# Output sums of a dense expert layer in three PSUM tiles instead of one of four banks

## The chip, the core and the metric

The kernel runs on one NeuronCore of a Trainium2 chip. The metric is the device time of one execution in microseconds (us). TensorE (PE in the profile) multiplies matrices and adds into PSUM; VectorE (DVE), ScalarE (ACT) and GpSimd (POOL) do the element-wise work; SyncE (SP) issues most DMAs. Each engine runs its own instruction stream in order and waits on semaphores where it needs another engine's result.

## What is computed

A local attention over 1536 tokens feeds a routed layer of 8 experts, and its output feeds a second, dense layer of 4 experts. The change touches the step between the two layers and the second layer:

```python
# first layer, cut: each token goes to one of 8 experts
for e in range(8):
    mask = expert_idx == e
    h = np.maximum(x[mask] @ w1[e], 0.0)
    out[mask] = gate_w[mask, None] * (h @ w2[e])
# second layer: every token through all 4 experts
p = domain_probs / (domain_probs.sum(-1, keepdims=True) + 1e-09)
for e in range(4):                            # w1 512 x 1024, w2 1024 x 512
    h = np.maximum(x @ w1[e], 0.0)
    out += p[:, e:e + 1] * (h @ w2[e])
```

## The kernel before

**Tiling.** The tokens are 12 row tiles of 128. Every float32 factor is split into a high and a low part (`hi`, `lo`), so one product of two blocks is three matmuls. In the second layer an expert is cut into two halves of its hidden width and the tokens into three groups of four row tiles; a half with a group is a **unit**, and there are 4 x 2 x 3 = 24 of them, u = 0 to 23. Inside a unit both layers' 2 x 2 block products are made with 7 products instead of 8 (Strassen's way), which gives seven hidden products and seven output products. I call them **H u.j** and **S u.j**, j = 0 to 6. Each is 12 matmuls of 128x256: H at L1046 to L1048, S at L1124 to L1126.

**Order.** The seven H of unit 0 come first, alone. Then for every unit the loop alternates S u.0, H u+1.0, S u.1, H u+1.1, ... S u.6, H u+1.6, so that a product of one kind covers the element-wise work of the other. The seven S of the last unit come alone at the end, in `final`. The order on each engine is the order in which the code is written.

**Around an S product.** `weigh` multiplies the two 128x256 halves of its sum by the expert's probability and adds them to `acc` (the tile `xall`): two DVE instructions at L1030, or ACT instructions at L1033 where a block of `acc` is touched first. In the last unit `row_out` then sends a row tile out by an indirect DMA from POOL (L1036). `rest(j)` makes inputs that later S products need: s3 by L1060, low parts by L1054 and L1057.

**Around an H product.** `hidden` forms sums of the seven products: ACT copies (L1077, L1079, L1083) and relus (L1085, L1093), DVE additions (L1082, L1090, L1092), and the inputs of S (L1051 high parts, L1057 and L1054 low parts, L1060 relu with a sum, L1096 a difference). They all stand in DVE's and ACT's queues among the weighs. A unit's H products use three PSUM tiles of one bank each, and one more bank is `e`.

**The output sums.** One PSUM tile `yp` of four banks holds the output sums of both layers. The first layer uses it as four blocks of 512 outputs' sums. In the second, `zs` hands out its four banks in turn, three for each unit: x, y and z. S u.0 opens x, S u.1 opens y, S u.2 opens z; j = 3, 4 and 6 add to x again, j = 5 to z. Waits between engines are placed by tile: an instruction that writes any bank of `yp` waits for every earlier reader of `yp`.

**Between the layers.** `rows_in(e)` loads an expert's place in the row order into a register of ACT and DVE (L860), copies the first partial sums from `yp` to x2 on ACT (L864, two of 128x512) and adds the second ones on DVE (L866, two). For the last expert it is called between H 0.1 and H 0.2. `between` spreads the rest over the steps: parts of x for the H products of the first units (`x_parts`, ACT L833 and DVE L834, kept in DRAM by `x_keep` and read back by `x_back`), and the preparation of the next weights (ACT L156, POOL L157). `makes` is the table that says after which step which part of x is made.

Of the kernel before, what the change touches and what calls it, by code (L numbers as in the profile page):

```python
# [11 lines left out]
F32 = mybir.dt.float32  # L12
# [5 lines left out]
ALU = mybir.AluOpType  # L18
# [4 lines left out]
P = 128  # L23
# [6 lines left out]
CAP = 256  # L30
WIDTHS = 184, 232, 256
# [5 lines left out]
def tile_attention_moe_moe(ctx: ExitStack, tc: tile.TileContext, q, k, v, n_global, n_local,  # L37
# [771 lines left out]
    with ExitStack() as mo:  # L809
# [17 lines left out]
        def x_parts(c):  # L827

            b11, b12, b21, b22 = (x_block(c, a_, b_) for a_ in (1, 2) for b_ in (1, 2))
            ta, tb = (x_block(0, 1, 1), x_block(0, 1, 2)) if c else (b11, b11)  # L830

            def op(j, src):
                nc.scalar.activation(xo[:, j, 0], src, AF.Copy)  # L833
                nc.vector.tensor_tensor(xo[:, j, 1], src, xo[:, j, 0].bitcast(F32), ALU.subtract)  # L834

            def sub(o_, a_, b_, eng=nc.vector):
                eng.tensor_tensor(o_, a_, b_, ALU.subtract)

            sums = [lambda eng: sub(ta, b12, b11, eng), lambda eng: sub(b12, b22, b12, eng), lambda eng: sub(tb, b22, ta, eng)]
# [18 lines left out]
        def rows_in(e):  # L858

            o_ = nc.values_load(offi[0:1, e:e + 1], engines=(mybir.EngineType.Activation, mybir.EngineType.DVE),  # L860
                                min_val=max(0, NT - (NE - e) * CAP), max_val=min(NT, e * CAP))
            rows = [x2[:, d:d + 2, bass.ds(o_, CAP)] for d in range(0, KD, 2)]
            for d in range(2):
                nc.scalar.copy(rows[d], yp[:, 2 * d:2 * d + 2, 0, :])  # L864
            for d in range(2):
                nc.vector.tensor_tensor(rows[d], yp[:, 2 * d:2 * d + 2, 1, :], rows[d], ALU.add)  # L866

        with ExitStack() as m1:
            mp1 = m1.enter_context(tc.tile_pool(name="mp1", bufs=1))
# [58 lines left out]
            parts = gate(mp1, rsrc)  # L928
            sorted_ = {}

            (sa, sb, sc_), ops = x_parts(0)
            first_parts = [ops[0], lambda: sa(nc.vector), lambda: sb(nc.vector), ops[1], lambda: sc_(nc.vector)] + ops[2:]
            xparts = {c: x_parts(c) for c in range(1, NCH)}

            def side(st):
# [34 lines left out]
            for e in range(NE):  # L970
                xa, xb = (xh, xl) if e else (xh0, xl0)
                for i in range(4):
                    st = 8 * e + i
                    wh, wl = use(st)
                    pt = next(hp)
                    for w_ in two_widths(wide) if e else (CAP,):
                        for f in range(2):
                            ws = slice(f * P, (f + 1) * P)
                            for c in range(KD):
                                o_, a_, b_ = pt[:, f, 0:w_], xa[:, c, 0:w_], xb[:, c, 0:w_]  # L980
                                nc.tensor.matmul(o_, wh[:, c, ws], a_, start=c == 0, stop=False)  # L981
                                nc.tensor.matmul(o_, wh[:, c, ws], b_, start=False, stop=False)
                                nc.tensor.matmul(o_, wl[:, c, ws], a_, start=False, stop=c == KD - 1)
                    relu3(pt, hhl[:, 2 * i:2 * i + 2, 0, :], hhl[:, 2 * i:2 * i + 2, 1, :])
                    split_to(min(st + PRE, W0))
                    side(st)
                    if st == 1:
                        nc.vector.memset(yp[:, :, :, WIDTHS[0]:], 0.0)
                for i in range(4):
                    st = 8 * e + 4 + i  # L990
                    wh, wl = use(st)
                    for f in range(2):
                        kf = 2 * i + f
                        for w_ in three_widths(wide):
                            a_ = hhl[:, kf, :, 0:w_]
                            for d in range(KD):
                                ws = slice(d * P, (d + 1) * P)
                                nc.tensor.matmul(yp[:, d, :, 0:w_], wh[:, f, ws], a_, start=kf == 0, stop=False, skip_group_check=True)  # L998
                                nc.tensor.matmul(yp[:, d, 0, 0:w_], wl[:, f, ws], a_[:, 0], start=False, stop=kf == KF - 1, skip_group_check=True)  # L999
                    if e + 1 < NE and i < 2:  # L1000
                        flip_x(e + 1, i)
                    if e + 1 < NE and i == 2:
                        ahead = wider(e + 1)
                    if i == 2 and e + 2 < NE:
                        load_x(e + 2)
                    split_to(min(st + PRE, W0))
                    side(st)
                wide = ahead
                if e < NE - 1:
                    rows_in(e)  # L1010


        with ExitStack() as m2:
            np1 = m2.enter_context(tc.tile_pool(name="np1", bufs=1))
            zs = cycle([yp[:, d] for d in range(KD)])
            LAST = 2 * NE2 - 1
            NU = NCH * 2 * NE2
            HT = CH // 2
# [43 lines left out]
            class Unit:  # L1062
# [65 lines left out]
                def second(self):  # L1128

                    n, t0 = self.n, self.t0  # L1130
                    t1_ = t0 + HT
                    x_, y_, z_ = (next(zs) for _ in range(3))
                    prods = ((x_, t0, 0), (y_, t0, 0), (z_, t1_, 1), (x_, t0, 1), (x_, t1_, 1), (z_, t0, 1), (x_, t1_, 0))
                    for j, (pt, t_, d_) in enumerate(prods):
                        for i in range(HT):
                            self.product(j, pt[:, i], i, j < 3 and i == 0)
                        for i in range(HT):
                            weigh(n, t_ + i, d_, pt[:, i])
                            if n == LAST and j > 4:
# [34 lines left out]
            def between(u, j):  # L1174

                n, c = divmod(u, NCH)
                if (u, j) in makes:
                    x_, m = makes[u, j]
                    xparts[x_][1][m]()
                    x_keep(x_, m)  # L1180
                if u == 0 and 4 <= j:
                    xparts[2][0][j - 4](nc.gpsimd)
                if u < 0 and j in (1, 4, 5, 6):
                    w2_op(0, j if j > 3 else 3)
# [222 lines left out]
```

## Time and profile before

| | us |
|---|---|
| median of three runs | 810.64 |
| lowest and highest | 809.51, 811.54 |
| the profiled execution | 807.23 |
| its span, first to last instruction | 805.2 |

All rows of the trace come from the profiled execution; 2.03 us of it lie outside the span. A row of the timeline gives the start, the duration, the engine, the line, what was written and read, and in brackets how long the engine had been idle before and what ended that. TensorE's matmuls overlap: one starts 0.12 us after another though each is recorded as 0.28 us, so "idle" begins later than the first possible start of the next. [...]

### The profile page before, as it was taken

How to read it: one execution, taken by the hardware profiler on the slowest of the kernel's cores; microseconds unless marked ns; L12 is line 12 of the kernel's file. 1: busy time of each engine (PE TensorE's matmuls, PEld its weight loads, DVE VectorE, ACT ScalarE, POOL GpSimd, SP SyncE). 2: the span in 40 equal slices, each digit the busy share in tenths (PEclk: the TensorE clock that was granted, in tenths of full speed). 3: DMA queues.
4: the chain of work that ended last, by engine and by line, in shares of the span. 5: the costliest groups of instructions: out<-in, count | busy, mean ns of one | idle time of the engine just before them, and what ended most of it. 6: DMA issues, size and time to landing. Idle time of an engine off the chain costs nothing. (4 is left out here: it accounts for less than half of the span.)

```text
span 805.2 us, 16423 instructions
## 1 busy us (share of the span) xinstructions
PE 756.6 (94%) x6267; PEld 729.5 (91%) x6267; DVE 561.3 (70%) x1186; ACT 427.7 (53%) x861; POOL 340.9 (42%) x313
## 2 busy tenths in 40 slices
PE   8999999999999888899999999999999999999983
PEld 5888899999999788899999999999999999999983
DVE  7888677778876577766667667667677667677652
ACT  7899477666755467653443453443454444354320
POOL 2036520340002663563564555356366266255252
PEclk9999999999999999999999999999999999999998
DMA  7986375676664754864566456466566466554602
GB/s 227 322 287 223 116 251 207 216 236 238 229 221 159 278 194 163 321 221 167 201 232 214 161 211 215 173 236 235 184 236 229 160 220 228 184 179 160 213 27 81
DMA packets 44418, 166.20 MB, mean 206 GB/s; under 512 B 5208, under 2 KB 11624, under 8 KB 36256
## 3 DMA queue, kind: packets, MB, share of 16 engines
q1 hardware_dynamic: 41888, 158.44, 55.9%
q0 software_dynamic: 2416, 6.39, 2.2%
q8 instruction: 66, 1.08, 0.5%
q14 instruction: 32, 0.26, 0.1%
q10 hardware_dynamic: 16, 0.02, 0.0%
HBM read 143.29 MB, written 21.54 MB: 205 GB/s over the span
## 5 line engine op out<-in xcount | busy, mean ns | idle before, releaser
L1124 PE MATMUL y<-wt,hp 128*128 128x256 f32 x672 | 193.1, 287 | 32.7 <-DVE xall L1030 19.9
L1030 DVE SCALAR_TENSOR_TENSOR xall<-y,rsb,xall 128x256 f32<-128x256 f32 x312 | 136.5, 479 | 108.1 <-PE y L1126 107.4
L1046 PE MATMUL h<-xo,wt 128*128 128x256 f32 x672 | 190.4, 283 | 3.0 <-ACT hf L1083 2.5
L1047 PE MATMUL h<-xo,wt 128*128 128x256 f32 x672 | 190.2, 283 | 0.0
L1125 PE MATMUL y<-wt,hp 128*128 128x256 f32 x672 | 190.1, 283 | 0.0
L1126 PE MATMUL y<-wt,hp 128*128 128x256 f32 x672 | 190.1, 283 | 0.0
L1048 PE MATMUL h<-xo,wt 128*128 128x256 f32 x672 | 190.0, 283 | 0.0
L157 POOL TENSOR_TENSOR wt<-raw,wt 128x512 fp32r<-128x512 f32 x75 | 98.0, 1307 | 166.1 <-ACT wt L156 164.6
L1124 PEld LDWEIGHTS y<-wt,hp 128*128 128x128 f32 x672 | 128.6, 191 | 39.3 <-ACT wt L156 12.6
L1046 PEld LDWEIGHTS h<-xo,wt 128*128 128x128 f32 x672 | 129.0, 192 | 3.4 <-ACT hf L1083 2.7
L1047 PEld LDWEIGHTS h<-xo,wt 128*128 128x128 f32 x672 | 129.0, 192 | 0.0
L1048 PEld LDWEIGHTS h<-xo,wt 128*128 128x128 f32 x672 | 129.0, 192 | 0.0
L1125 PEld LDWEIGHTS y<-wt,hp 128*128 128x128 f32 x672 | 128.8, 192 | 0.0
L1126 PEld LDWEIGHTS y<-wt,hp 128*128 128x128 f32 x672 | 128.8, 192 | 0.0
L1051 ACT ACTIVATE hp<-hf 128x512 fp32r<-128x512 f32 x120 | 75.4, 628 | 69.4 <-DVE hf L1060 68.0
L1054 DVE TENSOR_TENSOR hp<-hf,hp 128x512 fp32r<-128x512 f32 x92 | 87.2, 948 | 0.0
L998 PE MATMUL y<-hhl,wh 128*128 128x368 f32 (+2 forms) x256 | 80.6, 374 | 0.0
L94 DVE TENSOR_TENSOR wl<-raw,wh 128x1024 fp32r<-128x1024 f32 x60 | 72.6, 1225 | 0.1
L1093 ACT ACTIVATE hf<-h 128x512 f32<-128x512 f32 x24 | 14.3, 598 | 102.2 <-DVE h L1092 102.2
L124 ACT ACTIVATE wh<-raw 128x1024 fp32r<-128x1024 f32 x59 | 61.9, 1058 | 12.6 <-DMA raw<-in_moe_w_dram 10.6
L999 PE MATMUL y<-hhl,wl 128*128 128x184 f32 (+2 forms) x256 | 66.7, 261 | 0.0
L981 PE MATMUL h<-xh,wh 128*128 128x232 f32 (+1 forms) x224 | 61.9, 276 | 0.0
(217 smaller groups left out, 1488.4 us busy)
## 6 DMA issues: line engine op xcount, KB each, us to landing
raw<-in_moe_w_dram SPq DMA_DIRECT2D x96, 512.0 KB, 4.4
xo<-xd SPq DMA_DIRECT2D x42, 1024.0 KB, 5.2
xo<-xd SPq DMA_DIRECT2D x21, 1536.0 KB, 6.3
xd<-xo SPq DMA_DIRECT2D x21, 512.0 KB, 2.9
xs<-zt SPq DMA_DIRECT2D x4, 1024.0 KB, 6.2
xr<-xs SPq DMA_DIRECT2D x14, 256.0 KB, 4.8
v<-in_v_dram SPq DMA_DIRECT2D x12, 256.0 KB, 4.5
k<-in_k_dram SPq DMA_DIRECT2D x11, 256.0 KB, 5.0
```

What stands on the lines that cost most here:

```text
L94: eng.tensor_tensor(lo, r, hi.bitcast(F32), ALU.subtract)
L157: eng.tensor_tensor(t[:, 1], src, t[:, 0].bitcast(F32), ALU.subtract)
L998: nc.tensor.matmul(yp[:, d, :, 0:w_], wh[:, f, ws], a_, start=kf == 0, stop=False, skip_group_check=True)
L1030: nc.vector.scalar_tensor_tensor(a_, src, w_, a_, ALU.mult, ALU.add)
L1046: nc.tensor.matmul(pt[:, i], wh[:, d, ws], xh_[:, d], start=new and i == d == 0, stop=False, skip_group_check=True)
L1047: nc.tensor.matmul(pt[:, i], wh[:, d, ws], xl_[:, d], start=False, stop=False, skip_group_check=True)
L1048: nc.tensor.matmul(pt[:, i], wl[:, d, ws], xh_[:, d], start=False, stop=d == 1, skip_group_check=True)
L1051: nc.scalar.activation(parts[i][0], src, func)
L1054: eng.tensor_tensor(parts[i][1], src, parts[i][0].bitcast(F32), ALU.subtract)
L1124: nc.tensor.matmul(pt, hh[:, f, ts_], wh[:, f], start=new and f == 0, stop=False, skip_group_check=True)
L1125: nc.tensor.matmul(pt, hh[:, f, ts_], wl[:, f], start=False, stop=False, skip_group_check=True)
L1126: nc.tensor.matmul(pt, hl[:, f, ts_], wh[:, f], start=False, stop=f == 1, skip_group_check=True)
```

## The change

The tile `yp` becomes three: `ya` with two banks, `y2` and `y3` with one each; the first layer still uses all four banks. In the second layer units take turns: an even unit has x in `ya`, y in `y2`, z in `y3`, an odd one x in `y2`, y in `ya`. The second bank of `ya` is then unused. In `final` the last unit's x is held in two tiles of the H pool.

`rows_in` is split into `place`, `rows_copy` and `rows_add`, and each of the last two now has three instructions (one of 128x512, two of 128x256) instead of two. For the last expert the place is loaded before its second half, the copies stay after H 0.1, and the additions come after H 0.2. The memset of unused columns becomes four. The subtraction in the seventh part of x becomes a step of its own, on POOL for two of the three groups; `makes` and the preparation of weights in unit 0's H products are dealt out anew.

```diff
-        yp = ps_y.tile([P, KD, 2, CAP], F32, name="y")
+        ya = ps_y.tile([P, 2, 2, CAP], F32, name="ya")
+        yp = [ya[:, 0], ya[:, 1], *(ps_y.tile([P, 2, CAP], F32, name=f"y{d}") for d in (2, 3))]
...
-            ops = [lambda: op(0, b11), lambda: op(1, ta), lambda: op(2, tb), lambda: op(3, b21), lambda: op(4, b12),
-                   lambda: op(5, b22), lambda: (sub(b21, b21, tb), op(6, b21))]
+                    lambda eng: sub(b21, b21, tb, eng)]
+            ops = [lambda: op(0, b11), lambda: op(1, ta), lambda: op(2, tb), lambda: op(3, b21), lambda: op(4, b12),
+                   lambda: op(5, b22), lambda: op(6, b21)]
...
-            for d in range(2):
-                nc.scalar.copy(rows[d], yp[:, 2 * d:2 * d + 2, 0, :])
-            for d in range(2):
-                nc.vector.tensor_tensor(rows[d], yp[:, 2 * d:2 * d + 2, 1, :], rows[d], ALU.add)
+        ys = (0, 2, ya), (2, 3, yp[2].unsqueeze(1)), (3, 4, yp[3].unsqueeze(1))
+
+        def rows_copy(o_):
+            for d0, d1, y_ in ys:
+                nc.scalar.copy(x2[:, d0:d1, bass.ds(o_, CAP)], y_[:, :, 0, :])
+
+        def rows_add(o_):
+            for d0, d1, y_ in ys:
+                rows = x2[:, d0:d1, bass.ds(o_, CAP)]
+                nc.vector.tensor_tensor(rows, y_[:, :, 1, :], rows, ALU.add)
...
+                if e == NE - 1:
+                    last_place = place(e)
...
-            zs = cycle([yp[:, d] for d in range(KD)])
...
-                    x_, y_, z_ = (next(zs) for _ in range(3))
+                    x_, y_, z_ = (yp[2], yp[0], yp[3]) if self.u % 2 else (yp[0], yp[2], yp[3])
...
-                    x_ = [next(zs)[:, 0] for _ in range(HT)]
-                    y_, z_ = (next(zs) for _ in range(2))
+                    xa, _, xb = (ps_h.tile([P, 2, HC], F32, tag="h", name="h") for _ in range(3))
+                    x_ = [xa[:, 0], xb[:, 0]]
+                    y_, z_ = yp[2], yp[3]
...
-            makes = {}
-            for x_ in (1, 2):
-                for m in range(7):
-                    makes[(-1, 2 * m + 3) if x_ == 1 and m < 2 else (0, m + 5) if m < 2 else (x_ - 1, m - 2)] = x_, m
+            makes = {(-1, 3): [(1, 0)], (-1, 6): [(1, 1)], (0, 0): [(1, 2)], (0, 1): [(1, 3)], (0, 2): [(1, 4), (1, 5)], (0, 3): [(1, 6), (2, 0)],
...
                 if j == 1:
-                    rows_in(NE - 1)
+                    rows_copy(last_place)
+                if j == 2:
+                    rows_add(last_place)
```

On TensorE, at the boundary between unit 4 and unit 5 (end of H 5.6, start of S 5.0), the order before, with the semaphores that an instruction waits on; `h` is an H tile, `hp110` and `hp111` are the high and low part of h11, the input of S u.0:

```order
L1046 MATMUL h_6938<-xo_1742,wt_6486 128x256
L1047 MATMUL h_6938<-xo_1742,wt_6486 128x256
L1048 MATMUL h_6938<-xo_1742,wt_6486 128x256
L1124 MATMUL y_1737<-wt_6524,hp110_5806 128x256 [waits DVE_49,Activation_49]
L1125 MATMUL y_1737<-wt_6524,hp110_5806 128x256
L1126 MATMUL y_1737<-wt_6524,hp111_5807 128x256 [waits Pool_49]
```

The same place after:

```order
L1058 MATMUL h_6959<-xo_1744,wt_6507 128x256
L1059 MATMUL h_6959<-xo_1744,wt_6507 128x256
L1060 MATMUL h_6959<-xo_1744,wt_6507 128x256
L1136 MATMUL y2_1738<-wt_6545,hp110_5836 128x256 [waits Activation_49]
L1137 MATMUL y2_1738<-wt_6545,hp110_5836 128x256
L1138 MATMUL y2_1738<-wt_6545,hp111_5837 128x256 [waits Pool_49]
```

No instruction moves; the first S matmul of a unit no longer waits on DVE's semaphore.

On ACT, around the last expert's rows between H 0.1 and H 0.2, before (`hf_5800` and `hf_5801` are copies of H sums, `x` is x2, `offi` the experts' places):

```order
L1079 COPY hf_5801<-h 128x512
L860 TENSOR_LOAD offi
L860 ISA x2
L864 ISA
L864 COPY x_1741<-y 128x2x256
L864 ISA
L864 COPY x_1741<-y 128x2x256
L156 ACTIVATE wt<-raw 128x512
L1083 COPY hf_5800<-h 128x512
```

After:

```order
L1091 COPY hf_5831<-h 128x512
L868 ISA
L868 COPY x_1743<-ya 128x2x256
L868 ISA
L868 COPY x_1743<-y_1738 128x256
L868 ISA
L868 COPY x_1743<-y_1739 128x256
L156 ACTIVATE wt<-raw 128x512
L1095 COPY hf_5830<-h 128x512
```

The load of the place has gone from here to an earlier point, and a third copy stands ahead of the copy that follows H 0.2's partial sum.

On DVE at the same place, before (L1082 adds H 0.2's partial sum to H 0.0's):

```order
L866 ISA
L866 TENSOR_TENSOR x_1741<-y,x_1741 128x2x256
L866 ISA
L866 TENSOR_TENSOR x_1741<-y,x_1741 128x2x256
L1082 TENSOR_TENSOR h<-h,hf_5800 128x512
L834 TENSOR_TENSOR xo<-x_1741,xo 128x512
L1090 TENSOR_TENSOR e<-h,hf_5801 128x512
```

After:

```order
L1094 TENSOR_TENSOR h<-h,hf_5830 128x512
L873 ISA
L873 TENSOR_TENSOR x_1743<-ya,x_1743 128x2x256
L873 ISA
L873 TENSOR_TENSOR x_1743<-y_1738,x_1743 128x256
L873 ISA
L873 TENSOR_TENSOR x_1743<-y_1739,x_1743 128x256
L835 TENSOR_TENSOR xo<-x_1743,xo 128x512
L1102 TENSOR_TENSOR e<-h,hf_5831 128x512
```

The additions of the rows have moved behind the addition of the partial sum.

## Rows read from the trace of the kernel before

**Rows 1.** The page, busy time of TensorE: us (share of span) and instructions.

```profile
PE 756.6 (94%) x6267; PEld 729.5 (91%) x6267; DVE 561.3 (70%) x1186; ACT 427.7 (53%) x861; POOL 340.9 (42%) x313
```

**Rows 2.** Busy time by stretch: start:end, length, engines' busy us (instructions), clock, DMA.

```profile
108.00:268.00 160.00, 160.00 (x1241) 156.12 (x1240) 123.08 (x156) 105.07 (x155) 26.04 (x19) 1.00 0.64 214
...
267.90:374.67 106.77, 93.91 (x758) 91.30 (x757) 69.40 (x105) 59.65 (x115) 60.24 (x44) 1.00 0.62 231
374.67:778.68 404.01, 387.33 (x3192) 384.02 (x3193) 278.29 (x495) 173.88 (x313) 200.60 (x153) 1.00 0.55 199
778.68:796.58 17.90, 11.72 (x84) 10.41 (x84) 6.94 (x15) 2.03 (x4) 9.29 (x9) 1.00 0.16 60
```

**Rows 3.** Timeline at the start of S 5.0: start, us, engine, line, [idle before].

```profile
393.57 0.69 DVE L1060 SCALAR_TENSOR_TENSOR hf<-e,hf 128x512 f32<-128x512 f32 x1 [0.67 <-ACT hf L1093]
...
394.30 0.69 DVE L1096 TENSOR_TENSOR hf<-hf,hf 128x512 f32<-128x512 f32 x1
...
394.65 0.28 PE L1047 MATMUL h<-xo,wt 128*128 128x256 f32 x1
...
394.77 0.28 PE L1048 MATMUL h<-xo,wt 128*128 128x256 f32 x1
...
394.91 0.87 DVE L1030 SCALAR_TENSOR_TENSOR xall<-y,rsb,xall 128x256 f32<-128x256 f32 x2
...
395.36 0.58 ACT L1051 ACTIVATE hp<-h 128x512 fp32r<-128x512 f32 x1
...
395.92 0.35 PE L1124 MATMUL y<-wt,hp 128*128 128x256 f32 x1 [0.88 <-ACT hp L1051]
395.97 0.69 DVE L1057 SCALAR_TENSOR_TENSOR hp<-h,hp 128x512 fp32r<-128x512 f32 x1 [0.19 <-ACT hp L1051]
```

**Rows 4.** What TensorE waited for, 374.67 to 776: total us, times, longest.

```profile
PE y L1124 <- ACT hp L1051: 8.8, 10, 0.9
PE y L1124 <- DVE xall L1030: 7.9, 9, 0.9
```

**Rows 5.** The same list, 268 to 374.

```profile
PE y L1124 <- DVE xall L1030: 5.0, 6, 1.6
PE y L1124 <- ACT xall L1033: 4.0, 4, 1.3
PE h L1046 <- ACT hf L1083: 2.5, 1, 2.5
PE h L1046 <- DVE e L1090: 0.6, 1, 0.6
```

**Rows 6.** Timeline around the last expert's rows, before H 0.4.

```profile
272.55 1.07 ACT L864 COPY x<-y 128x512 f32 x2 [0.97 <-issue]
...
273.65 1.29 DVE L866 TENSOR_TENSOR x<-y,x 128x512 f32 x2 [5.65 <-ACT x L864]
...
274.86 0.69 DVE L1082 TENSOR_TENSOR h<-h,hf 128x512 f32<-128x512 f32 x1
...
276.27 0.38 PE L1046 MATMUL h<-xo,wt 128*128 128x256 f32 x1 [2.45 <-ACT hf L1083]
```

**Rows 7.** Instructions that read tile y, ACT at L1033: duration min/median/max in ns.

```profile
L1033 ACT ACTIVATE xall<-y,rsb x24: 454/467/477, 285.0 to 352.9; 128x256 f32<-128x256 f32 x24
```

**Rows 8.** What TensorE waited for, 776 to 800.

```profile
PE y L1124 <- DVE xall L1030: 7.1, 7, 1.1
```

**Rows 9.** Timeline of the end: POOL's row_outs, the last matmul, the last weigh.

```profile
784.19 0.99 POOL L1036 DMA_INDIRECT out_dram<-xall,rsb  x1 [0.15 <-issue]
785.49 0.98 POOL L1036 DMA_INDIRECT out_dram<-xall,rsb  x1 [0.30 <-issue]
...
796.30 0.28 PE L1126 MATMUL y<-wt,hp 128*128 128x256 f32 x1
796.62 0.48 DVE L1030 SCALAR_TENSOR_TENSOR xall<-y,rsb,xall 128x256 f32<-128x256 f32 x1 [1.79 <-PE y L1126]
...
798.66 0.98 POOL L1036 DMA_INDIRECT out_dram<-xall,rsb  x1 [0.31 <-POOLq L1226]
```

More of the change, by code (lines that the diff above doesn't have):

```diff
@@ L837, in sub @@
                 eng.tensor_tensor(o_, a_, b_, ALU.subtract)
-            sums = [lambda eng: sub(ta, b12, b11, eng), lambda eng: sub(b12, b22, b12, eng), lambda eng: sub(tb, b22, ta, eng)]
+            sums = [lambda eng: sub(ta, b12, b11, eng), lambda eng: sub(b12, b22, b12, eng), lambda eng: sub(tb, b22, ta, eng),
+                    lambda eng: sub(b21, b21, tb, eng)]
             ops = [lambda: op(0, b11), lambda: op(1, ta), lambda: op(2, tb), lambda: op(3, b21), lambda: op(4, b12),
-                   lambda: op(5, b22), lambda: (sub(b21, b21, tb), op(6, b21))]
+                   lambda: op(5, b22), lambda: op(6, b21)]
             return sums, ops
@@ L856, in relu3, with place @@
             nc.vector.scalar_tensor_tensor(lo, pt, 0.0, hi.bitcast(F32), ALU.max, ALU.subtract)
[L858 to L862, printed above, removed]
-            for d in range(2):
-                nc.scalar.copy(rows[d], yp[:, 2 * d:2 * d + 2, 0, :])
-            for d in range(2):
-                nc.vector.tensor_tensor(rows[d], yp[:, 2 * d:2 * d + 2, 1, :], rows[d], ALU.add)
+        def place(e):
+            return nc.values_load(offi[0:1, e:e + 1], engines=(mybir.EngineType.Activation, mybir.EngineType.DVE),
+                                  min_val=max(0, NT - (NE - e) * CAP), max_val=min(NT, e * CAP))
+        ys = (0, 2, ya), (2, 3, yp[2].unsqueeze(1)), (3, 4, yp[3].unsqueeze(1))
[6 more added lines that the diff above has]
+                nc.vector.tensor_tensor(rows, y_[:, :, 1, :], rows, ALU.add)
         with ExitStack() as m1:
@@ L929, in tile_attention_moe_moe @@
             sorted_ = {}
-            (sa, sb, sc_), ops = x_parts(0)
-            first_parts = [ops[0], lambda: sa(nc.vector), lambda: sb(nc.vector), ops[1], lambda: sc_(nc.vector)] + ops[2:]
+            sums_, ops = x_parts(0)
+            sums_ = [lambda f=f: f(nc.vector) for f in sums_]
+            first_parts = [ops[0], *sums_[0:2], ops[1], sums_[2], *ops[2:4], sums_[3], *ops[4:]]
             xparts = {c: x_parts(c) for c in range(1, NCH)}
@@ L987, in tile_attention_moe_moe @@
                     if st == 1:
-                        nc.vector.memset(yp[:, :, :, WIDTHS[0]:], 0.0)
+                        for y_ in yp:
+                            nc.vector.memset(y_[:, :, WIDTHS[0]:], 0.0)
+                if e == NE - 1:
+                    last_place = place(e)
                 for i in range(4):
@@ L997, in tile_attention_moe_moe @@
                                 ws = slice(d * P, (d + 1) * P)
-                                nc.tensor.matmul(yp[:, d, :, 0:w_], wh[:, f, ws], a_, start=kf == 0, stop=False, skip_group_check=True)
-                                nc.tensor.matmul(yp[:, d, 0, 0:w_], wl[:, f, ws], a_[:, 0], start=False, stop=kf == KF - 1, skip_group_check=True)
+                                nc.tensor.matmul(yp[d][:, :, 0:w_], wh[:, f, ws], a_, start=kf == 0, stop=False, skip_group_check=True)
+                                nc.tensor.matmul(yp[d][:, 0, 0:w_], wl[:, f, ws], a_[:, 0], start=False, stop=kf == KF - 1, skip_group_check=True)
                     if e + 1 < NE and i < 2:
@@ L1009, in tile_attention_moe_moe @@
                 if e < NE - 1:
-                    rows_in(e)
+                    o_ = place(e)
+                    rows_copy(o_)
+                    rows_add(o_)
         with ExitStack() as m2:
             np1 = m2.enter_context(tc.tile_pool(name="np1", bufs=1))
-            zs = cycle([yp[:, d] for d in range(KD)])
             LAST = 2 * NE2 - 1
@@ L1176, in between @@
                 n, c = divmod(u, NCH)
-                if (u, j) in makes:
-                    x_, m = makes[u, j]
+                for x_, m in makes.get((u, j), ()):
                     xparts[x_][1][m]()
                     x_keep(x_, m)
[L1181 to L1184, printed above, removed]
+                if u in (0, 1) and j == 2:
+                    xparts[u + 1][0][3](nc.gpsimd)
+                if u == 0 and 3 <= j < 6:
+                    xparts[2][0][j - 3](nc.gpsimd)
+                if u < 0:
+                    for m in {1: (3,), 4: (4,), 6: (5, 6)}.get(j, ()):
+                        w2_op(0, m)
                 if NCH <= u + 2 < NU and j in (2, 4, 6):
@@ L1202, in between @@
                     w1_op(n + 1, 6)
-            makes = {}
-            for x_ in (1, 2):
-                for m in range(7):
-                    makes[(-1, 2 * m + 3) if x_ == 1 and m < 2 else (0, m + 5) if m < 2 else (x_ - 1, m - 2)] = x_, m
+            makes = {(-1, 3): [(1, 0)], (-1, 6): [(1, 1)], (0, 0): [(1, 2)], (0, 1): [(1, 3)], (0, 2): [(1, 4), (1, 5)], (0, 3): [(1, 6), (2, 0)],
+                     (0, 4): [(2, 1)], (1, 0): [(2, 2)], (1, 1): [(2, 3)], (1, 2): [(2, 4)], (1, 3): [(2, 5)], (1, 4): [(2, 6)]}
             unit = Unit(0)
```

## The prediction

> **What bounds the kernel now.** I read the page's shares first, then busy time by stretch, then the list of what TensorE waited for in each stretch, and single boundaries in the timeline last. TensorE is busy 94% of the span [rows 1]; where the rest goes is told by the stretches [rows 2]. In the first layer (108 to 268) TensorE is busy 160.00 of 160 us, at clock 1.00: nothing can be won there. The second layer is cut at its first matmul (267.90), at the first matmul of S 4.0 (374.67) and at that of S 23.0 (778.68). Two matmuls in a row start 0.12 us apart (394.65, 394.77 [rows 3]), so a product of 12 takes 1.44 us and the matmuls alone set a floor for each stretch:
>
> - head, 267.90 to 374.67: 106.77 us for 63 products = 756 matmuls x 0.12 = 90.72. Lost: 16.05.
> - steady part, 374.67 to 778.68: 404.01 us for 19 units of 168 matmuls, 383.04. Lost: 20.97, or 1.10 a unit.
> - tail, 778.68 to the last matmul's start at 796.30 [rows 9]: 17.62 us for 83 steps of 0.12, 9.96. Lost: 7.66.
>
> Together 44.68 us: all that a change of TensorE's waits can win.
>
> Who ends the waits? In the steady part there are 19, one for each unit, all ahead of an S product, 0.88 us each [rows 4]. The list puts ten of them down to ACT's L1051, but at S 5.0 that instruction runs from 395.36 to 395.94 and the matmul starts at 395.92 [rows 3]: it can't be the cause. The weigh of S 4.6 can: DVE does it from 394.91 to 395.78, 0.14 before the matmul. It is late because it stands in DVE's queue behind L1060 and L1096 (393.57 to 394.99), which make inputs from H 5.5. S 5.0 writes another bank than the weigh reads, but the same tile, so it waits. The listing of TensorE before shows that wait on DVE; the listing after does not have it. S 5.0 could start at 394.89; it starts 1.03 later, and its first matmul takes 0.20 to the next instead of 0.12, together the 1.10.
>
> In the head ten waits out of twelve are of the same kind, 9.0 us of idle [rows 5]; one, 2.5 us, is that of H 0.4, one, 0.6, that of H 0.6. The idle time, 12.1 us, is less than the loss of 16.05, since a wait costs about 0.22 more than its idle (0.88 against 1.10) and short delays leave no idle at all. In the tail seven S products run with no H between, and each waits for the weigh before it, 7.1 us [rows 8].
>
> **The change, part by part.**
>
> Steady part. Between units the wait for the weigh of S u-1.6 goes: S u.0 now opens a tile that was last read by the weigh of S u-1.1, a whole unit ago. What is late next? S u.1 opens the tile that S u-1.6 used and waits for that same weigh: it ends at 395.78, and S 5.1 would start at 394.89 + 2.88 = 397.77, so 2.0 are to spare. S u.3, u.4 and u.6 write x again and wait for the weigh of x's product before. From the last matmul's start to the end of its weighs it takes 0.32 + 0.87 (796.30 to 796.62 [rows 9], and the pair in [rows 3]) = 1.19; an H product of 1.44 lies between, and so S may start 1.56 after that matmul: 0.37 to spare. In the trace every S u.1 to u.6 has this wait already, since all banks are one tile, and none of the 19 waits stands there. Next is DVE's own row. With t0 = 394.77, the last matmul of H 5.6: weighs to 395.78, L1057 395.97 to 396.66, another L1060 to 397.34, the weighs of S 5.0 (0.87) to 398.2, L1060 for s3 to 398.9 at the latest; H 6.1, which takes over the PSUM tile that s3 is made from, would start at 394.89 + 3 x 1.44 = 399.21. That leaves 0.3 to 0.55, so nothing is lost as long as these rows keep their length. DVE is busy 278.29 us in the stretch [rows 2], and 383.04 remain. I take the whole 20.97; at the least half, 10.5, if that row comes up short by 0.55 in each unit.
>
> Tail. The order there is j = 0, 1, 2, 3, 5, 4, 6. Each product waits for a weigh that lies at least two products back, but for S 23.6, which adds to x right behind S 23.4; there x's two halves have a tile each, and the weigh of the one (0.48) can run under the matmuls of the other. TensorE would take 9.96 plus little. But POOL follows: its row_outs start 1.30 apart (784.19, 785.49), the first two don't depend on the last unit's sums, and with four more at that distance the last starts at 784.19 + 5 x 1.30 = 790.69 and not at 798.66 [rows 9]. That wins 7.97. The weighs keep up: the last product would end near 787.8, its weighs near 788.9, and the row_outs that need them stand at 789.39 and 790.69. Of the 7.97, S 23.0's own late start (1.03) is already in the steady part's sum. The tail gives 6.9; the ends are 6 and 7.6.
>
> Head. The ten waits for weighs and the short delays cost 16.05 less 2.8 for H 0.4 and 0.8 for H 0.6, 12.4. They go as in the steady part, but ACT does some of these weighs, among parts of x that the new table packs closer (two in one step, twice); I leave 0.4 for S 0.4 and 1.1 for the rest: 10.9 won. H 0.4 waits for a chain: 0.97 of ACT's idle for the load of the place, two copies, DVE's two additions (273.65 to 274.94), L1082 behind them, a copy on ACT, then the matmul at 276.27 [rows 6]. H 0.3 is through 2.6 us earlier. After the change the load is gone from here and L1082 stands ahead of the additions; what remains is a third copy on ACT and a weight's preparation, so about 0.5 of 2.8 stays: 2.3 won. The wait of H 0.6 stays. Head: 13.2; the ends are 10 and 15.
>
> Small parts. Three copies and three additions instead of two: a 128x256 copy from this tile takes 467 ns on ACT [rows 7] and one of 128x512 some 540 in a row (1.07 for two [rows 6]), so 0.4 more on ACT; on DVE 2 x 0.48 for 0.65, 0.3 more. For seven experts this lies in the first layer, where ACT is busy 105.07 and DVE 123.08 of 160 us [rows 2]: taken at nothing, at most 7 x 0.3 = 2 if TensorE waited for it each time, and the early load of the place at most its 0.97. Four memsets for one, and a subtraction that moves to POOL: nothing, POOL being busy 60.24 of 106.77 in the head.
>
> The sum: 20.97 + 6.9 + 13.2 = 41.1. On the profiled execution 807.23 - 41.1 = 766.1. The median of the three runs is 3.41 above that execution, so **769.5**.
>
> **The rivals.**
>
> B, the wait moves inside the unit. If DVE's row or the weigh of x is late by the 0.3 to 0.5 that I count as spare, H u.1 or S u.4 waits in each of 20 units; with half of the boundary's gain lost: 769.5 + 10.5 = 780. For it: the slack is thinner than one DVE instruction (0.69). Against it: all instructions of that row are of one length wherever I looked, and S u.1 to u.6 wait for nothing today. [...]
>
> C, the head keeps its loss. The new table brings two parts of x in a step on ACT and DVE, and three copies stand ahead of L1083's successor. If the head wins 3 and not 13.2: about 780 too.
>
> D, the waits don't go: another wait on DVE takes the place at each boundary, 807 to 811 as before. The listing speaks against it: S u.0 waits for ACT alone, for h11's high part, which was made from H u.3 three steps ago.
>
> [...]
>
> **How the numbers follow.** What a measurement of this kernel can tell from no change is about 0.3%, 2.4 us. The forecast (765 to 775) has 0.72, B 0.12, C 0.08, D 0.03, E 0.03, and 0.02 is left for what I don't see. The range takes in the forecast with all that the matmuls' gaps could give (810.64 - 44.68 = 766.0, less 1), and the centres of B and C at 780 with 2 us more: 765 to 782. Faster 0.95 (forecast, B, C and most of the rest), same 0.02 (most of D), slower 0.03 (E).
>
> **What would show it.** In the profile after: no wait of S u.0 for L1042 (the weigh), units 20.16 us apart and not 21.27, H 0.4 less than 1 us late, S 23.1 to S 23.6 1.44 apart, and the last six row_outs in one row 1.3 apart. [...]

## The result and the profile after

The changed kernel takes **774.03 us** (median of 4 runs, 773.41 to 775.57), the kernel before 810.89 in runs on the same chip: a ratio of 0.955 with a 95% interval of 0.953 to 0.957. The forecast was 769.5 with a range of 765 to 782. The time lies in the range, and it is 4.5 above the forecast; on the profiled executions the shortfall is larger, 7.3 (see the total, below).

The profiled execution after took 773.41 us with a span of 771.7. Cut at the same places as in [rows 2], its stretches read (first the length, then busy us of PE, PEld, DVE, ACT, POOL, then TensorE's granted clock as a share of full speed):

```profile
268.74:368.41 99.67, 93.91 (x758) 91.55 (x757) 73.41 (x101) 57.59 (x114) 66.74 (x46) 1.00 0.66 248
368.41:751.45 383.04, 383.04 (x3194) 383.04 (x3193) 279.82 (x495) 172.56 (x313) 201.90 (x152) 1.00 0.57 209
```

| | before | after | won | forecast |
|---|---|---|---|---|
| up to the first H matmul | 267.90 | 268.74 | -0.84 | 0 |
| head, to S 4.0 | 106.77 | 99.67 | 7.10 | 13.2 |
| steady part, to S 23.0 | 404.01 | 383.04 | 20.97 | 20.97 |
| tail, to the end of the last row_out | 20.96 | 14.03 | 6.93 | 6.9 |
| behind it | 5.56 | 6.22 | -0.66 | 0 |
| span | 805.2 | 771.7 | 33.5 | 41.1 |

The steady part is at its floor to the hundredth: TensorE is busy 383.04 of 383.04 us at clock 1.00, and the list of what it waited for from 374 to the end is empty. The boundary that [rows 3] show reads, in the timeline after:

```profile
388.45 0.28 PE L1060 MATMUL h<-xo,wt 128*128 128x256 f32 x1
388.57 0.28 PE L1136 MATMUL y<-wt,hp 128*128 128x256 f32 x1
```

and on DVE at the same place:

```profile
388.59 0.87 DVE L1042 SCALAR_TENSOR_TENSOR xall<-ya,rsb,xall 128x256 f32<-128x256 f32 x2
389.65 0.69 DVE L1069 SCALAR_TENSOR_TENSOR hp<-h,hp 128x512 fp32r<-128x512 f32 x1 [0.19 <-ACT hp L1063]
390.26 0.68 DVE L1072 SCALAR_TENSOR_TENSOR hf<-h,hf 128x512 f32<-128x512 f32 x1
390.86 0.86 DVE L1042 SCALAR_TENSOR_TENSOR xall<-y,rsb,xall 128x256 f32<-128x256 f32 x2
391.64 0.68 DVE L1072 SCALAR_TENSOR_TENSOR hf<-h,hf 128x512 f32<-128x512 f32 x1
```

The weigh of S 4.6 (L1042 reading `ya`) starts when S 5.0 (writing `y2`) already runs. The row on DVE goes on to s3, which ends at 392.32; H 6.1 starts at 392.89.

What is missing is in the head. The list of TensorE's waits there, 268 to 374 (us, times, longest), to be held against [rows 5]:

```profile
PE y L1138 <- DVE hp L1066: 1.6, 1, 1.6
PE ya L1136 <- DVE xall L1042: 1.3, 1, 1.3
PE ya L1136 <- ACT hp L1063: 0.8, 1, 0.8
PE h L1058 <- DVE e L1102: 0.7, 1, 0.7
PE y L1136 <- ACT hp L1063: 0.7, 1, 0.7
...
```

From matmul start to matmul start the head loses 8.95 us. In the order of the program: H 0.4 0.29, H 0.6 0.97, H 1.3 to S 0.5 2.5 (the 1.6 of the list in it), S 0.6 1.56, S 1.1 1.50, S 2.1 1.44, H 4.1 0.37, some 0.3 in pieces.

### The profile page after: what moved, and what is told of

Read it like the earlier page. It is cut to its first block, busy times and chain, and to the rows that moved or that the text cites. A ratio compares the mean times of both kernels' runs of the same rounds, so it can differ in the third digit from the quotient of the medians.

```text
span 771.7 us, 16432 instructions
## 1 busy us (share of the span) xinstructions
PE 751.9 (97%) x6267; PEld 729.0 (94%) x6267; DVE 569.0 (74%) x1195; ACT 425.5 (55%) x869; POOL 349.4 (45%) x315
## 5 line engine op out<-in xcount | busy, mean ns | idle before, releaser
L157 POOL TENSOR_TENSOR wt<-raw,wt 128x512 fp32r<-128x512 f32 x75 | 101.5, 1354 | 148.8 <-ACT wt L156 148.5
L1042 DVE SCALAR_TENSOR_TENSOR xall<-y,rsb,xall 128x256 f32<-128x256 f32 x198 | 86.2, 476 | 48.5 <-PE y L1138 48.5
L1138 PE MATMUL y<-wt,hp 128*128 128x256 f32 x420 | 119.0, 283 | 1.8 <-DVE hp L1066 1.6
L1136 PE MATMUL y<-wt,hp 128*128 128x256 f32 x420 | 119.0, 283 | 0.7 <-ACT hp L1063 0.7
L1137 PE MATMUL y<-wt,hp 128*128 128x256 f32 x420 | 118.8, 283 | 0.0
L1066 DVE TENSOR_TENSOR hp<-hf,hp 128x512 fp32r<-128x512 f32 x92 | 92.9, 1010 | 0.0
L1138 PEld LDWEIGHTS y<-wt,hp 128*128 128x128 f32 x420 | 80.6, 192 | 2.2 <-DVE hp L1066 1.8
L1136 PEld LDWEIGHTS y<-wt,hp 128*128 128x128 f32 x420 | 80.6, 192 | 0.9 <-ACT hp L1063 0.9
L1137 PEld LDWEIGHTS y<-wt,hp 128*128 128x128 f32 x420 | 80.6, 192 | 0.0
L1136 PE MATMUL ya<-wt,hp 128*128 128x256 f32 x236 | 67.0, 284 | 2.1 <-DVE xall L1042 1.3
L1138 PE MATMUL ya<-wt,hp 128*128 128x256 f32 x236 | 67.0, 284 | 0.2 <-DVE hp L1069 0.2
L1137 PE MATMUL ya<-wt,hp 128*128 128x256 f32 x236 | 66.8, 283 | 0.0
```

The source lines that it names most:

```text
L157: eng.tensor_tensor(t[:, 1], src, t[:, 0].bitcast(F32), ALU.subtract)
L1042: nc.vector.scalar_tensor_tensor(a_, src, w_, a_, ALU.mult, ALU.add)
L1066: eng.tensor_tensor(parts[i][1], src, parts[i][0].bitcast(F32), ALU.subtract)
L1136: nc.tensor.matmul(pt, hh[:, f, ts_], wh[:, f], start=new and f == 0, stop=False, skip_group_check=True)
L1137: nc.tensor.matmul(pt, hh[:, f, ts_], wl[:, f], start=False, stop=False, skip_group_check=True)
L1138: nc.tensor.matmul(pt, hl[:, f, ts_], wh[:, f], start=False, stop=f == 1, skip_group_check=True)
```

## The experiments

Each was run beside the kernel before. Its medians on the chips of the experiments were 808.0 to 808.8, below the 810.89 above, so ratios are compared; the stretches come from the profile of each run. The median is of 4 runs.

| run | median us | ratio (95%) | head | steady part |
|---|---|---|---|---|
| changed kernel | 774.03 | 0.955 (0.953 to 0.957) | 99.67 | 383.04 |
| after_again | 772.02 | 0.956 (0.954 to 0.958) | 99.69 | 383.04 |
| a_one_tile | 799.77 | 0.991 (0.989 to 0.992) | 106.66 | 402.86 |
| b_split_only | 771.94 | 0.956 (0.955 to 0.958) | 99.01 | 383.04 |
| c_four_tiles | 771.84 | 0.956 (0.954 to 0.958) | 99.68 | 383.04 |
| d_spread | 770.12 | 0.954 (0.952 to 0.956) | 97.40 | 383.04 |
| e_two_more | 793.30 | 0.981 (0.980 to 0.983) | 104.74 | 402.00 |
| f_hi1_later | 772.09 | 0.956 (0.953 to 0.959) | 95.48 | 387.17 |
| g_best | 774.05 | 0.957 (0.956 to 0.959) | 96.26 | 387.15 |
| i_adds_early | 770.69 | 0.953 (0.952 to 0.955) | 98.19 | 383.04 |
| j_hi1_first_units | 767.50 | 0.949 (0.948 to 0.951) | 97.10 | 383.03 |
| k_and_tail | 767.02 | 0.950 (0.948 to 0.952) | 95.23 | 383.04 |
| l_final_one_tile | 776.15 | 0.960 (0.958 to 0.961) | 101.19 | 384.07 |

### One tile again

```diff
-        ya = ps_y.tile([P, 2, 2, CAP], F32, name="ya")
-        yp = [ya[:, 0], ya[:, 1], *(ps_y.tile([P, 2, CAP], F32, name=f"y{d}") for d in (2, 3))]
+        yt = ps_y.tile([P, KD, 2, CAP], F32, name="y")
+        ya = yt[:, 0:2]
+        yp = [yt[:, d] for d in range(KD)]
```

> The changed kernel with its three output tiles joined again into one tile of four banks; the turn of the banks, the two H tiles for the last unit's x and all other edits stay. Theory 1 (the waits by tile are the loss): every S u.0 waits for the weigh of S u-1.6 again, units are 21.27 us apart and not 20.16, the steady part gets its 20.97 us back, the head 6 to 10; the tail stays bound by POOL's row_outs, 0 to 3. So 774.0 + 27 to 34 = 801 to 808. Theory 2 (a good part of the gain comes from the other edits, the moved additions and the new table): under 795.

Measured: 799.77, some 28 us above what the changed kernel's ratio gives on that chip. The banks and their turn are the same as after; only the tile is one. TensorE's waits from 374 to 770 are those of [rows 4] again:

```profile
PE y L1137 <- DVE xall L1043: 8.7, 10, 0.9
PE y L1137 <- ACT hp L1064: 7.9, 9, 0.9
```

The steady part is 19.8 us longer than after (18 boundaries of 1.10; the one before S 23.0 is gone, since x of the last unit stays in the H tiles), the head 7.0, and the last row_out ends 15.0 after S 23.0 against 14.0. So the loss hangs on the tile, not on the bank. The time is 1.2 under the lowest figure of Theory 1, but the kernel before was 2.9 faster on this chip; as a difference, 28 lies in its 27 to 34. Its 20.97 has one boundary too many. The head's 7.0 is no clean measure: 1.6 of it is a later H 0.6 and some 2.8 are matmuls at a lower clock (0.97 over the head), both told of at the end.

### The split alone

The kernel before with this and what hangs on it: an expert's rows in three copies and three additions, still in one go, four memsets, and the last unit's x in two H tiles. Its own table of the parts of x stays.

```diff
-        yp = ps_y.tile([P, KD, 2, CAP], F32, name="y")
+        ya = ps_y.tile([P, 2, 2, CAP], F32, name="ya")
+        yp = [ya[:, 0], ya[:, 1], *(ps_y.tile([P, 2, CAP], F32, name=f"y{d}") for d in (2, 3))]
...
-                    x_, y_, z_ = (next(zs) for _ in range(3))
+                    x_, y_, z_ = (yp[2], yp[0], yp[3]) if self.u % 2 else (yp[0], yp[2], yp[3])
```

> The kernel before with the output sums in three tiles, the turn of units and the last unit's x in H tiles; the last expert's rows in one go before H 0.2 and the old table of parts of x stay. Theory 1: steady part 383.04 and tail as in the changed kernel; in the head H 0.4 waits 2.5 us longer, while the two waits that follow the packed parts of x (S 0.5 and S 0.6, 3.4 us in the changed kernel) shrink, so 772 to 778. Theory 2 (the other edits carry weight of their own beyond that): over 780.

Measured: 0.956, the same as the whole change. The head is 99.01 against 99.67 to 99.69: H 0.4 waits 2.36, the waits at S 0.5 and S 0.6 are not there, and H 2.0 waits 1.77 in their place. All other edits together are worth nothing that can be measured: the moved additions and the early load win 2.1 at H 0.4, and the new table loses as much (d_spread, below, is 2.3 shorter in the head without it).

### Four tiles in turn

```diff
-        ya = ps_y.tile([P, 2, 2, CAP], F32, name="ya")
-        yp = [ya[:, 0], ya[:, 1], *(ps_y.tile([P, 2, CAP], F32, name=f"y{d}") for d in (2, 3))]
+        yp = [ps_y.tile([P, 2, CAP], F32, name=f"y{d}") for d in range(KD)]
...
-                    x_, y_, z_ = (yp[2], yp[0], yp[3]) if self.u % 2 else (yp[0], yp[2], yp[3])
+                    x_, y_, z_ = (next(zs) for _ in range(3))
```

> The changed kernel with four output tiles of one bank each, handed out in turn, so that no bank is idle (four copies and four additions of 128x256 for an expert's rows). Theory 1: three are enough, since no wait is left in the steady part: units 20.16 us apart, time within 1 us of 774.0. [...]

Measured: head 99.68 and steady part 383.04, with the same waits at the same products as after. The idle bank costs nothing: three tiles are enough.

### The changed kernel once more

> The changed kernel unaltered, beside the kernel before on this chip, as a base for the runs of this call. Theory 1 (the 1 us of idle in the first layer at 166 to 170 us, which no wait for the change's own instructions ends, belongs to that execution): the first matmul of the second layer is back at 267.4 to 267.9 and the time is 0.955 of before less 1 us. Theory 2 (the program's new layout makes it): 268.7 again.

Measured: the first matmul of the second layer is at 267.96, and head, steady part and tail agree with the first profile within 0.02. Of the first profile's 0.84 nothing is left; the other eleven runs had it between 267.43 and 268.06 too. It belonged to that execution.

### The parts of x one at a step

```diff
-            makes = {(-1, 3): [(1, 0)], (-1, 6): [(1, 1)], (0, 0): [(1, 2)], (0, 1): [(1, 3)], (0, 2): [(1, 4), (1, 5)], (0, 3): [(1, 6), (2, 0)],
-                     (0, 4): [(2, 1)], (1, 0): [(2, 2)], (1, 1): [(2, 3)], (1, 2): [(2, 4)], (1, 3): [(2, 5)], (1, 4): [(2, 6)]}
+            makes = {}
+            for x_ in (1, 2):
+                for m in range(7):
+                    makes[(-1, 2 * m + 3) if x_ == 1 and m < 2 else (0, m + 5) if m < 2 else (x_ - 1, m - 2)] = [(x_, m)]
```

> The changed kernel with the old table of the parts of x: one part at a step, at H 0.3 and H 0.5 and at S 0.0 to S 0.6. Theory 1 (packing two parts into a step makes the low part for S 0.5 and the weigh before S 0.6 late): those two waits, 3.4 us, shrink to under 1; 771. Theory 2 (the additions on DVE are slow beside GpSimd's work, 1.7 us each instead of 0.7, wherever they stand): the delay moves on to S 0.6, S 1.0 and S 1.1, 773 to 776.

Measured: the waits at S 0.5 and S 0.6 go from 3.36 to 0.13, as Theory 1 had it, and S 1.1 no longer waits. But H 2.0, which reads the first part of x for unit 2, now waits 1.77: half of the delay moves on, as Theory 2 had it, though not to the places that it named. Head 97.40, 2.3 better than after. The rows of DVE in the changed kernel show why packing costs so much:

```profile
291.96 3.47 DVE L835 TENSOR_TENSOR xo<-x,xo 128x512 fp32r<-128x512 f32 x2
295.35 1.75 DVE L1066 TENSOR_TENSOR hp<-hf,hp 128x512 fp32r<-128x512 f32 x1
297.02 3.48 DVE L835 TENSOR_TENSOR xo<-x,xo 128x512 fp32r<-128x512 f32 x2
300.42 0.86 DVE L1042 SCALAR_TENSOR_TENSOR xall<-ya,rsb,xall 128x256 f32<-128x256 f32 x2
```

The two parts ahead of the low part for S 0.5 (L1066) take 3.47, the two ahead of the weigh for S 0.6 (L1042) 3.48. Without POOL beside it such an instruction takes 0.69 (at 302.94 in d_spread).

### The additions ahead of the partial sum again

On top of the last one:

```diff
                 if j == 1:
                     rows_copy(last_place)
-                if j == 2:
                     rows_add(last_place)
```

> The run with the old table of parts of x, and the last expert's additions again ahead of H 0.2's partial sum on DVE; the place is still loaded early and there are three copies. Theory 1 (H 0.4 waited for the load, 0.97, and for the additions, together): three additions of 0.69, 0.48 and 0.48 put the partial sum 1.3 to 1.6 later, so H 0.4 is 1.3 to 1.6 later and the head that much longer, 0.7 of it perhaps hidden by later waits. Theory 2 (the load alone was it): H 0.4 stays 0.2 to 0.3 late, no change.

Measured: H 0.4 is 1.21 late against 0.28, 0.93 more, less than the 1.3 to 1.6 expected. In b_split_only, where the place is also loaded at the old point, it is 2.36. So of the 2.71 before the additions' place is worth 0.9 and the early load up to 1.15 (the two runs differ in small edits beside it), and both theories named half of it. The head is 0.8 longer, which the time doesn't show (0.953 against 0.954).

### Two more instructions on DVE at each unit's start

```diff
-                        relu_and(s4, self.b, s2, ALU.subtract)
+                        for _ in range(3):
+                            relu_and(s4, self.b, s2, ALU.subtract)
```

> The changed kernel with the instruction that makes s4 on DVE at each unit's start repeated twice more (0.60 us each in a row, same result). Theory 1 (DVE's row from the weighs of S u-1.6 to s3 stands just under TensorE's limit): it ends 0.57 us before H u.1 in two units of three and 0.82 in the third, of which 0.15 are needed, so 1.20 more costs 0.78 in 13 and 0.53 in 6 of 19 steady units, 13 us, and units of 20.9 and 20.7; with the first units 13 to 16 us slower than the changed kernel, the wait standing at H u.1. Theory 2 (DVE, busy 73% of the steady part, has room there): under 3 us slower.

Measured (against the changed kernel): the steady part is 19.0 us longer, not 13, with 1.09 at H u.1 in two units of three and 0.84 in the third. The theory holds and its price was short: the same output written again takes 0.72 a time (three in 2.13), not 0.60. The two cost 1.45, and 1.45 less the spare 0.42 and 0.67 gives the late starts of 1.02 and 0.77 that the trace shows. The waits are all at the place named:

```profile
PE h L1058 <- DVE hf L1072: 14.7, 19, 0.9
```

DVE has 100 us to spare in this part of the kernel, and 0.42 us where it counts.

### The high part of s1 later on ACT

On top of the parts of x one at a step:

```diff
                         relu_and(s1, self.e, h12, ALU.add)
-                        hi(1, s1)
...
                         hi(12, self.b, AF.Relu)
+                        hi(1, s1)
                         lo_relu(12, self.b)
```

> The run with the old table of parts of x, and with the high part of s1 on ACT behind that of h12 (S u.2 needs the one, S u.1 the other). Theory 1 (S 1.1, S 2.1 and H 2.0 wait because ACT does the first-touch weigh of S u.6 late, behind the high part of s1, and the high part of h12 behind that): H 2.0 waits 0.5 us less, S 2.1 0.6 less, 1 to 2 us faster than that run. Theory 2 (the part of x on DVE sets it): within 0.5 us.

Measured: H 2.0 waits 1.29 and not 1.77, S 2.1 0.54 and not 1.42, and the head is 1.9 shorter, though H 0.6 is 1.6 later in this profile (below). Theory 1 holds in the head, but the time is no shorter (0.956 against 0.954). The last row_out ends 15.3 after S 23.0 and not 14.0, because POOL's low part of s1 waits for the later high part. And the steady part is 4.1 longer: H u.1 loses 0.34 in 12 units, and the cause is on DVE:

```profile
382.48 1.68 DVE L1107 TENSOR_TENSOR hf<-hf,hf 128x512 f32<-128x512 f32 x1
```

and on POOL:

```profile
382.32 1.29 POOL L157 TENSOR_TENSOR wt<-raw,wt 128x512 fp32r<-128x512 f32 x1 [1.11 <-ACT wt L156]
```

With one instruction fewer ahead of it, ACT's L156 comes early, POOL's L157 starts with it, and beside it DVE's difference for s2 takes 1.68 where [rows 3] have 0.69 for the same instruction. The margin of 0.42 is used up in these units; in the third group the two do not meet (0.69 at 423.49).

### Parts of x earlier still

On top of the last one:

```diff
-                    makes[(-1, 2 * m + 3) if x_ == 1 and m < 2 else (0, m + 5) if m < 2 else (x_ - 1, m - 2)] = [(x_, m)]
+                    makes[((-1, (3, 5, 6)[m]) if m < 3 else (0, m - 3)) if x_ == 1 else (0, m + 4) if m < 3 else (1, m - 3)] = [(x_, m)]
...
-                elif c == 0 and j == 3:
+                elif (u, j) == (1, 0) or c == 0 and j == 3 and u:
                     w2_sums(n + 1)
```

> As the run with the high part of s1 later, and two moves more: the parts of x of groups two and three each one step earlier, still one at a step, from H 0.3, H 0.5 and H 0.6 on, and GpSimd's sums for the next half's second weights behind S 1.0 and not behind S 0.3. Theory 1 (what is left in the head is parts of x on DVE late at H 2.0, slowed by GpSimd beside it): H 2.0's wait of 1.8 us goes, 2 to 3 us faster than that run. Theory 2 (the load only moves): a wait at S 0.0 to S 0.2 takes its place, within 1 us.

Measured: H 2.0's wait of 1.29 goes, and S 1.1 (0.38) and H 2.1 (0.65) wait in its place, so most of the load only moves, as Theory 2 had it, though not to the places that it named. The head is not shorter (96.26), but 2.0 us at H 0.6 and 1.1 in the matmuls of S 0.0 come from the late write and the lower clock that are told of at the end, so what these moves are worth by themselves stays open. The steady part and the tail have the losses of the run before.

### Later in the first units alone, and the low part of s3 on DVE

On top of the parts of x one at a step:

```diff
-                        hi(1, s1)
+                        if not 0 < self.u < NCH + 1:
+                            hi(1, s1)
...
                         hi(12, self.b, AF.Relu)
+                        if 0 < self.u < NCH + 1:
+                            hi(1, s1)
```

> The run with the old table of parts of x, and the high part of s1 behind that of h12 on ACT for units 1 to 3 alone, where ACT still does first-touch weighs. Theory 1 (in the run that did it for all units the head gained and two steady units in three lost 0.33 at H u.1, because the row on DVE that ends in s3 slipped over its margin of 0.42): the steady part is 383.04 again, the head 94 to 95.5, so 2 to 3.5 us faster than the run with the old table alone. Theory 2 (the steady loss has another cause): 387 in the steady part.

Measured: the steady part is 383.03 again, and the ratio is 0.949 against the changed kernel's 0.955 and 0.956: faster than both kernels, by some 0.6% against the changed one if the ratios are compared. The profiled head is 97.10, longer than expected, because H 0.6 loses 3.8, a wait and slower matmuls behind it that are told of below; the next run, with the same instructions in the head, loses 1.0 there and has a head of 95.23.

On top of this:

```diff
-                    lo(3, s3, nc.gpsimd)
                     for t_ in late:
...
+                        if j == 2:
+                            lo(3, s3)
```

> As the run with the high part of s1 later in units 1 to 3, and the low part of s3 in the last unit made on DVE, not on GpSimd. Theory 1 (GpSimd's chain sets the end): the first row_outs start 1.3 earlier, then the weighs of S 23.5 hold them; the last row_out ends 0.5 to 1.0 sooner after S 23.0. Theory 2 (TensorE and the last weigh set the end): no change.

Measured: the ratio is the same (0.950), and the last row_out ends 13.99 after S 23.0 against 14.00 to 14.03. The first row_outs come earlier, as expected, and then POOL waits for the weighs of S 23.5, which itself starts 0.9 late: the weigh of S 23.2, whose tile it writes, stands on DVE behind the low part of s3. Theory 1's gain of 0.5 to 1.0 is not there. So a row of POOL that starts earlier wins nothing, while in f_hi1_later one that started 1.3 later cost 1.3.

### The last unit's x in one tile

Against the changed kernel:

```diff
-                    xa, _, xb = (ps_h.tile([P, 2, HC], F32, tag="h", name="h") for _ in range(3))
-                    x_ = [xa[:, 0], xb[:, 0]]
+                    x_ = [ya[:, 0, 0], ya[:, 1, 0]]
```

> The changed kernel with the last unit's x in the two banks of ya, one tile, and not in two tiles of the H pool. Theory 1 (GpSimd's chain sets the end, with a margin): S 23.6 waits for both weighs of S 23.4, 0.9 to 1.2 more, and the weighs of S 23.6 come that much later, still ahead of the row_outs that need them at 11.8 and 13.0 after S 23.0: the last row_out ends 14.0 after S 23.0 as before, time within 0.4 of the changed kernel's 772 to 774. Theory 2 (the two tiles carry part of the tail's gain): about 1 us slower.

Measured: 0.960, 3 us or more slower if the ratios are compared. Theory 2 was right in kind and short in size. Two waits came back. S 23.0 waits again for the weigh of S 22.6, which reads ya; the expectation had left that out. And S 23.6 waits for both weighs of S 23.4, after which POOL waits too:

```profile
765.46 0.98 POOL L1048 DMA_INDIRECT out_dram<-xall,rsb  x1 [1.83 <-DVE xall L1042]
766.74 0.98 POOL L1048 DMA_INDIRECT out_dram<-xall,rsb  x1 [0.30 <-POOLq L1240]
```

The last row_out ends 14.57 after S 23.0, which is 1.03 late itself, together 1.6 more than after. The two H tiles are part of the tail's gain. The head of this profile is 1.5 longer too, with the late H 0.6 and the lower clock told of at the end; whether all four runs had them is not known.

## Why the prediction was right, and where it fell short

**Steady part: right in kind and size.** The wait was for the weigh of S u-1.6, through the tile; ACT's L1051, which the list named ten times, was not it. The split takes all 20.97 us without the moved additions and the new table (b_split_only), and joining the tiles puts back 1.10 at every boundary but the one whose tile stayed apart (a_one_tile). The margin of DVE's row was put at 0.3 to 0.55; the trace shows 0.57 and 0.82 from the end of s3 to H u.1, and e_two_more prices it at 0.42 and 0.67.

**Tail: right.** 6.93 against 6.9, with six row_outs in a row on POOL as described:

```profile
758.06 0.99 POOL L1048 DMA_INDIRECT out_dram<-xall,rsb  x1 [0.15 <-issue]
759.36 0.98 POOL L1048 DMA_INDIRECT out_dram<-xall,rsb  x1 [0.30 <-issue]
760.64 0.98 POOL L1048 DMA_INDIRECT out_dram<-xall,rsb  x1 [0.30 <-issue]
761.93 0.98 POOL L1048 DMA_INDIRECT out_dram<-xall,rsb  x1 [0.30 <-DVE xall L1042]
763.21 0.98 POOL L1048 DMA_INDIRECT out_dram<-xall,rsb  x1 [0.30 <-POOLq L1241]
764.50 0.98 POOL L1048 DMA_INDIRECT out_dram<-xall,rsb  x1 [0.30 <-issue]
```

That POOL alone sets the end was too much said: f_hi1_later shows POOL's row setting it, but k_and_tail and l_final_one_tile show the weighs close behind.

**Head: the mis-sized term.** It was to win 13.2 and won 7.1. H 0.4 (0.29 left, 0.5 forecast), H 0.6 (0.97, stays) and S 0.4 (0.14, 0.4 forecast) came as written. The step that failed is "and 1.1 for the rest": the rest is 7.5. Of it 3.4 are at S 0.5 and S 0.6, where the new table has two parts of x in a step and each of these takes 1.74 on DVE beside POOL and not 0.7 (d_spread takes the 3.4 away and pays 1.8 at H 2.0). Another 2.9 are at S 1.1 and S 2.1: with the wait at S u.0 gone, S u.1 comes early enough to meet the high part of h12, which stands on ACT behind a first-touch weigh and the high part of s1. With that part later, S 2.1's wait falls from 1.42 to between 0.5 and 0.7 (j_hi1_first_units, k_and_tail). For S 1.1 the cause is less firmly shown: its wait had already gone where H 2.0 waits ahead of it (d_spread), and with the part later and H 2.0 on time it is 0.38 and not 1.50 (g_best). The cause of the last 1.2 (H 1.3, H 1.4, H 4.1 and pieces) stays open.

The prediction saw the packing (rival C) but gave no row for its 1.1. The trace before had one, in the list of DVE's instructions from 268 to 374:

```profile
L834 DVE TENSOR_TENSOR xo<-x,xo 128x512 fp32r<-128x512 f32 x14 | 12.8, 913 | 12.1 <-ACT xo L833 12.1
```

The instruction that makes a part of x took 913 ns on average there, not the 0.69 us of the instructions of that size in [rows 3], and the new table puts two of them ahead of a product. And of S u.1 the prediction asked only what its tile waits for, not when its input, the high part of h12, is ready while ACT still does the weighs.

**Rivals.** B did not come: nothing in the steady part waits, and a fourth tile in turn, which leaves no bank idle (c_four_tiles), changed the head by 0.01 and the steady part by nothing. C came in part: the head won 6.1 us less where C had 10, and the packing that C names is 3.4 of the loss. D did not. Nor did E, a kernel that gets slower because TensorE is granted a lower clock in the second layer: the steady part's 383.04 us without a gap ran at clock 1.00, and so did the head.

**The total.** On the profiled executions the change is 33.8 us and the sum had 41.1: 6.1 from the head, 0.84 from an execution's own delay in the first layer, 0.66 behind the last row_out, less 0.3 outside the span. That the median lies only 4.5 above the forecast is in part luck. The forecast put 3.41 on top for the step from the profiled execution to the median, as before the change; after it this step is 0.62. On the medians the change is 36.9.

## What to carry to other kernels

Where an engine waits at a regular place for something in another part of the same PSUM tile, split the tile: the wait goes by the tile and not by the bank, and the whole gap (here 1.10 us a unit) can go if the next wait in line has room. Work out that next wait for the first units by their own queues, since the engine that does the weighs there is another one, and ask of each product when its input is ready, not only its tile. And where DVE and POOL work side by side, take the lengths of DVE's instructions with two SBUF inputs from a stretch where both are busy (here 1.74 us, and 0.69 with POOL idle).

## What the runs showed of the hardware

**DVE beside POOL.** The same DVE instruction (L1066, 128x512, both inputs in SBUF) takes 1.75 us at 295.35 and, with POOL idle,

```profile
309.89 0.68 DVE L1066 TENSOR_TENSOR hp<-hf,hp 128x512 fp32r<-128x512 f32 x1
```

while at 295.35 POOL was in this one:

```profile
294.84 1.71 POOL L838 TENSOR_TENSOR x<-x 128x512 f32<-128x512 f32 x1
```

It ends 0.55 after POOL's, and so does L1107 in f_hi1_later (384.16 after 383.61). Weighs, which have an input in PSUM, keep their length beside POOL: two take 0.86 at 300.42, where POOL's L838 runs from 299.91 to 302.88, and 0.87 at 312.32, where POOL is idle. How POOL's instruction holds up DVE's is not shown.

**A write that lands late.** H 0.6 starts 0.8 to 1.0 late in eight of the fourteen profiles and 2.6 to 3.3 in six, namely a_one_tile, e_two_more, f_hi1_later, g_best, j_hi1_first_units and l_final_one_tile. In these six ACT's part of x waits 2.17 to 2.87 for the DMA that keeps the part before it in DRAM, here in j_hi1_first_units:

```profile
277.71 0.63 ACT L834 ACTIVATE xo<-x 128x512 fp32r<-128x512 f32 x1 [2.50 <-DMA xd<-xo]
```

and in k_and_tail, with the same instructions around it, ACT does not wait:

```profile
275.34 0.63 ACT L834 ACTIVATE xo<-x 128x512 fp32r<-128x512 f32 x1
```

What delays the write stays open.

**A lower clock behind a wait.** Behind that wait, TensorE's granted clock in j_hi1_first_units fell to 0.50 of full speed (281.00 to 282.30), and its matmuls started 0.21 apart and not 0.12. The columns are those of [rows 2]:

```profile
276.00:279.70 3.70, 1.07 (x9) 0.87 (x8) 1.32 (x3) 1.15 (x2) 1.34 (x2) 1.00 1.03 421
279.70:281.00 1.30, 1.27 (x7) 1.27 (x8) 0.64 (x2) 0.60 (x1) 1.30 (x2) 0.60 1.02 416
281.00:282.30 1.30, 1.30 (x8) 1.30 (x8) 1.27 (x2) 0.64 (x2) 0.44 (x1) 0.50 1.03 419
282.30:284.00 1.70, 1.70 (x12) 1.70 (x12) 1.21 (x3) 1.70 (x4) 0.00 (x0) 0.68 0.58 236
284.00:286.00 2.00, 2.00 (x20) 2.00 (x19) 2.00 (x4) 2.00 (x6) 1.59 (x2) 1.00 0.85 295
```

TensorE had waited 2.66 us there. The clock fell in the same way in a_one_tile, g_best (0.54 from 281.00 to 284.00) and l_final_one_tile, after waits of 2.37, 2.48 and 2.76 ahead of H 0.6, and once more in a_one_tile after one of 2.85 ahead of S 0.5: over the head it is 0.97 there and 0.98 in j_hi1_first_units. Over the whole span it is 0.992 in a_one_tile and 0.993 in g_best, j_hi1_first_units and l_final_one_tile, where f_hi1_later and e_two_more have 0.997 and 0.998. It did not fall after 2.45 ahead of H 0.4 in [rows 6] (1.00 from 276.27 to 278.00), nor ahead of H 0.6 after 2.32 in f_hi1_later (1.00 over the head) and 3.02 in e_two_more (1.00 from 279.70 to 284.00). So the length of the wait alone does not decide it, and what does is not shown.
